# First MLP's weight words: a sign made on GpSimd, third k/v buffer pair, and q loads placed later in the plan

## The chip, the cores and the metric

One core of a Trainium2 chip runs the whole kernel. The metric is the device time of one execution in microseconds (us); three executions of the kernel before are shown and their median is used. Engines in the rows: PE is TensorE (PEld its weight loads), DVE is VectorE, ACT is ScalarE, POOL is GpSimd, SP is the engine whose queue issues nearly all DMAs.

## The reference, cut to what matters

```python
q_s = softmax(q, axis=-1)            # per row, over 64 features
k_s = softmax(k, axis=2)             # per feature, over 576 positions
kv = einsum('bhsd,bhse->bhde', k_s, v)
x = einsum('bhsd,bhde->bhse', q_s, kv)   # -> (4608, 512)
h = x @ w_in;  x = relu(h) ** 2 @ w_out          # first MLP, 512 -> 2048 -> 512
g = x @ w_gate; y = (g * sigmoid(g) * (x @ w_val)) @ w_out2   # second MLP, 512 -> 1536 -> 512
```

Batch 8, heads 8, sequence 576, head size 64. The three attention inputs are float32; the weights of both MLPs are float64 and reach the kernel as 64-bit words.

## The kernel before, in words

**Stages.** The 4608 rows are nine blocks of 512 (NB = 9). In the first half of the kernel the attention and the first MLP run block by block; the second half is the second MLP, whose products are written as seven instead of eight (the tiles `ps`, `wu`, `xo`, `uo`). Every matrix product of the MLPs is three float32r matmuls (`mm3`, L107): each operand is split into a rounded high part and the rest (`split`, L103), and high x high, high x low, low x high are added up.

**First MLP.** For block i and slice f of the 2048 hidden features (NF = 16 slices of 128) `h_mm` (L439) makes h in the PSUM tile `ph` with 12 matmuls, `g_of` (L446) makes relu squared and splits it (ScalarE: `r`, `r`, `g`; VectorE: the low half of `g`), and one slice later `acc_mm` (L454) adds the slice to the four accumulators `acc`, 12 matmuls again. So a slice is 24 matmuls.

**Weight words.** In block 0 the 32 weight slices of the first MLP (16 of `w_in`, 16 of `w_out`, 128 x 512 values of 64 bits each) are loaded, converted and split while the block is computed; later blocks find them ready. `Weights.step` (L193) is called after the prologue twice per slice f. One step does three things: `split` of the slice converted in the step before (ScalarE copy L189, GpSimd subtract L191), `bits` of the next one, and `load` (L162) of one more on SP's queue, about three steps ahead of its use. `bits_of` (L125) turns 64-bit words into float32 bit patterns: ScalarE scales the high word, read as a float32, by 2**-112 into a PSUM tile `pa` (L138); VectorE shifts it left by 3 and masks the sign bit (L140), ors in the three top bits of the low word (L144) and ors in the sign of the high word (L148, result `wbits` in SBUF). With `psum=False` the same function serves the second MLP's weights, which are converted later in blocks 1 to 7; there the intermediate tile is in SBUF. The raw words of the 32 slices are loaded into slots that the split weights take later (pools `wpa`, `wpb`); the pool `raws` (two tiles `wraw` of 4 KB a partition) is used by the second MLP's weights alone, which start in block 1.

**Attention, planned by ticks.** Work of the next block's attention is laid between the slices: the main loop calls `tick(2f)` and `tick(2f + 1)` for each f, and `attention_plan(i)` (L422) says at which tick a piece starts; a piece is a generator that advances one step per tick. For pair hp of heads (four pairs), `load_kv` (L295) loads k into the tile `kt` (one buffer) and v into `vt` (one tile), two ticks before `kv_unit` (L318), which starts at tick 2, 9, 16 or 26. `kv_unit` ends its reads of `kt` and `vt` with the 24 small matmuls of L345. `load_q` (L307) loads q into `qs` (two buffers) four ticks before `q_unit` (L359), which starts at tick 11, 12, 17 and 20, so q is loaded at ticks 7, 8, 13 and 16. The transposes `q_transpose` (L376, matmuls of L380) of pairs 0 and 1, which free the two `qs` buffers, are at ticks 14 and 16. Batch 0 and block 0 are handled by a prologue of their own (L693 to L726), with borrowed buffers.

**Order of the work.** SP's queue is issued in the order of the program (L688); an issue that must wait for a buffer holds everything behind it. The instructions of the other engines are put into an order at build time by the framework's scheduler, which looks at readiness and at the order of the program; at run time each engine works in its order and a waiting instruction holds those behind it.

Of the kernel before, what the change touches and what calls it, by code (L numbers as in the profile page):

```python
# [8 lines left out]
F32 = mybir.dt.float32  # L9
# [3 lines left out]
ALU = mybir.AluOpType  # L13
# [4 lines left out]
P = 128  # L18
# [4 lines left out]
def tile_linear_attention_two_mlps(  # L23
# [29 lines left out]
    nc = tc.nc  # L53
    B, H, S, D = q.shape
# [3 lines left out]
    T = 512  # L58
# [6 lines left out]
    CK = 96  # L65
    NC = S // CK
    LAG = 1

    def f32(ap):
        return ap.bitcast(F32)  # L70
# [15 lines left out]
    raws = ph0.enter_context(tc.tile_pool(name="raws", bufs=2, side="right"))  # L86
# [38 lines left out]
    def bits_of(raws_, psum=False):  # L125

        todo = []  # L130
        for raw in raws_:
            low, high = (
                raw.bitcast(I32).rearrange("p (n t) -> p n t", t=2)[:, :, t] for t in (0, 1)
            )
            w = cv.tile([P, T], I32, name="wbits", tag="wbits")
            todo.append((low, high, w, ps_a.tile([P, T], I32, name="pa", tag="pa") if psum else w))
        for low, high, w, t in todo:
            nc.scalar.activation(f32(t), f32(high), AF.Copy, scale=2.0**-112)  # L138
        for low, high, w, t in todo:
            nc.vector.tensor_scalar(  # L140
                t, t, 3, 0x7FFFFFFF, op0=ALU.logical_shift_left, op1=ALU.bitwise_and
            )
        for low, high, w, t in todo:
            nc.vector.scalar_tensor_tensor(  # L144
                t, low, 29, t, op0=ALU.logical_shift_right, op1=ALU.bitwise_or
            )
        for low, high, w, t in todo:
            nc.vector.scalar_tensor_tensor(  # L148
                w, high, -2**31, t, op0=ALU.bitwise_and, op1=ALU.bitwise_or
            )  # L150
        return [f32(w) for low, high, w, t in todo]

    class Weights:
# [22 lines left out]
        def bits(self, n):  # L176
            keys = self.order[self.n_bits:min(self.n_bits + n, self.n_load)]
            for key, w in zip(keys, bits_of([self.raw.pop(key) for key in keys], True)):
                self.mid[key] = w
            self.n_bits += len(keys)  # L180
# [33 lines left out]
    def operands(kind, f):  # L214
# [3 lines left out]
        for s in (f, NG + f):  # L218
            t = raws.tile([P, T], w.dtype, name="wraw", tag="wraw")
            raw_load(w, by_rows, s, t)  # L220
            raw.append(t)
        yield
        first, = bits_of(raw[:1])
        yield
        second, = bits_of(raw[1:])
        yield
        a, b = first[:, 0:U], first[:, U:2 * U]
# [50 lines left out]
    kts, qs, qT, xT = {}, {}, {}, {}  # L278

    def load_k(b, hp, t=None):  # L280
        if t is None:
            t = kp.tile([CK, 2, NC, D], F32, name="kt", tag="kt")
        nc.sync.dma_start(t, k[b, 2 * hp:2 * hp + 2].rearrange("h (p c) d -> p h c d", c=NC))
        return t

    def load_v(b, hp, t=None):
        if t is None:
            t = vt1
        for h in range(2):
            nc.sync.dma_start(  # L290
                t[:, h, :, 0:D], v[b, 2 * hp + h].rearrange("(p c) d -> p c d", c=NC)
            )
        return t

    def load_kv(b, hp):  # L295
        kts[b, hp] = load_k(b, hp), load_v(b, hp)

    def runs(i):

        done = 0  # L300
        while done < T:
            b, s = divmod(i * T + done, S)
            n = min(T - done, S - s)
            yield done // TJ, n // TJ, b, s
            done += n

    def load_q(i, hp, t=None):  # L307
        if t is None:
            t = qp.tile([P, TJ, 2, D], F32, name="qs", tag="qs")
        for p0, n, b, s in runs(i):  # L310
            for h in range(2):
                nc.sync.dma_start(
                    t[p0:p0 + n, :, h, :],
                    q[b, 2 * hp + h, s:s + n * TJ, :].rearrange("(p j) d -> p j d", j=TJ),
                )
        qs[i, hp] = t
# [42 lines left out]
    def q_unit(i, hp):  # L359

        t = qs.pop((i, hp))
        m = sp.tile([P, TJ, 2], F32, name="qm", tag="qm")
        nc.vector.tensor_reduce(m, t, axis=AX.X, op=ALU.max, negate=True)  # L363
        yield
        for j in range(TJ):
            for h in range(2):
                nc.scalar.activation(t[:, j, h], t[:, j, h], AF.Exp, bias=m[:, j, h:h + 1])  # L367
        yield
        r = sp.tile([P, TJ, 2], F32, name="qr", tag="qr")
        nc.vector.tensor_reduce(r, t, axis=AX.X, op=ALU.add)  # L370
        nc.vector.tensor_scalar(r, r, EPS, None, op0=ALU.add)
        nc.vector.reciprocal(r, r)  # L372
        nc.gpsimd.tensor_tensor(t, t, r.unsqueeze(3).to_broadcast([P, TJ, 2, D]), op=ALU.mult)  # L373
        qs[i, hp] = t

    def q_transpose(i, hp, t=None):  # L376
        pt = ps_a.tile([P, T], F32, name="pa", tag="pa")
        src = qs.pop((i, hp)).rearrange("p j h d -> p j (h d)")
        for j in range(TJ):
            nc.tensor.transpose(pt[:, j * P:(j + 1) * P], src[:, j], ident)  # L380
        if t is None:
            t = qtp.tile([P, 2, T], F32R, name="qT", tag="qT")
        split(t[:, 0], t[:, 1], pt)
        qT[i, hp] = t
# [16 lines left out]
    def run_at(plan):  # L401

        table = {}

        def add(n, fn):
            table.setdefault(n, []).append(fn)

        for n, make in plan:
            add(n, make)
        live = []  # L410

        def tick(n):
            nonlocal live
            live = [g for g in live if next(g, 0) is None]
            for make in table.get(n, ()):
                g = make()
                if g is not None and next(g, 0) is None:
                    live.append(g)

        return tick  # L420

    def attention_plan(i):  # L422

        plan = []
        if i < B:
            for hp, n in enumerate((2, 9, 16, 26)):
                plan.append((max(n - 2, 0), lambda hp=hp: load_kv(i, hp)))
                plan.append((n, lambda hp=hp: kv_unit(i, hp)))
        if i < NB:
            for hp, n in enumerate((11, 12, 17, 20)):  # L430
                plan.append((n - 4, lambda hp=hp: load_q(i, hp)))
                plan.append((n, lambda hp=hp: q_unit(i, hp)))
            plan.append((14, lambda: q_transpose(i, 0)))
            plan.append((16, lambda: q_transpose(i, 1)))
        return run_at(plan)
# [252 lines left out]
    with tc.manual_schedule(engines={mybir.EngineType.SP}):  # L688
# [4 lines left out]
        def borrowed():  # L693
            return f32(w_slot(wpb)).rearrange("p t n -> p (t n)")

        for hp in range(NP):
            kt = borrowed()[:CK, 0:2 * NC * D].rearrange("p (h c d) -> p h c d", h=2, c=NC)
            vt = borrowed()[:CK, 0:2 * NC * (D + 1)].rearrange("p (h c d) -> p h c d", h=2, c=NC)
# [3 lines left out]
        for what in "k0 k1 q0 v0 k2 q1 k3 v1 w v2 w q2 q3 w v3".split():  # L702
# [3 lines left out]
            hp = int(what[1])  # L706
# [7 lines left out]
        plan = []  # L714
# [15 lines left out]
        for n in range(NB * NF + LAG):  # L730
            i, f = divmod(n, NF)
            a = divmod(n - LAG, NF) if n >= LAG else None
            if i < NB:
                if f == 0:
                    for hp in range(NP if i else 0):
                        x_pair(i, hp)
                        if hp + 2 < NP:
                            q_transpose(i, hp + 2)
                        acc_mm(*a, hp)
                    tick = attention_plan(i + 1)  # L740
                    if i == NB - 1:
                        for _ in work:
                            pass
                        ph0.close()
                        for name, bufs in (("x1", 14), ("wr", EARLY), ("xs", 5)):
                            pools[name] = ctx.enter_context(
                                tc.tile_pool(name=name, bufs=bufs, side="right", reuse_waits="tile")
                            )
                        prime()
                        xo = XOperands(0)  # L750
                        xo.load(0)
                        for _ in range(EARLY):
                            stream.fetch()
                ph = h_mm(i, f)
                tick(2 * f)
                g_of(i, f, ph)
                if i == 0:
                    w1.step(1)
                elif i < NB - 1 and n >= NF + 2:
                    next(work, None)  # L760
# [68 lines left out]
```

## Time and profile before

| | |
|---|---|
| executions shown | 1717.01, 1717.17, 1723.07 us; median 1717.17 us |
| the profiled execution | 1724.42 us; its span 1721.9 us |
| busy in the span | PE 1687.8, DVE 919.6, ACT 861.8, POOL 253.9 us |
| first MLP's block 0, from its first steady matmuls to the end | 39 to 145 us of the span |

The rows of a trace are read as follows. A group of instructions is named by its source line, engine, operation and tiles (out<-in). A timeline row gives start, duration, count, and in brackets how long the engine was idle before and which instruction ended the wait. A row of windows gives for a stretch the busy time of each engine, the granted clock of TensorE as a share of full speed, the DMA engines' load and rate.

### The profile page before, as it was taken

How to read it: one execution, taken by the hardware profiler on the slowest of the kernel's cores; microseconds unless marked ns; L12 is line 12 of the kernel's file. 1: busy time of each engine (PE TensorE's matmuls, PEld its weight loads, DVE VectorE, ACT ScalarE, POOL GpSimd, SP SyncE). 2: the span in 40 equal slices, each digit the busy share in tenths (PEclk: the TensorE clock that was granted, in tenths of full speed). 3: DMA queues.
4: the chain of work that ended last, by engine and by line, in shares of the span. 5: the costliest groups of instructions: out<-in, count | busy, mean ns of one | idle time of the engine just before them, and what ended most of it. 6: DMA issues, size and time to landing. Idle time of an engine off the chain costs nothing.

```text
span 1721.9 us, 25446 instructions
## 1 busy us (share of the span) xinstructions
PE 1687.8 (98%) x9414; PEld 1435.6 (83%) x9414; DVE 919.6 (53%) x1626; ACT 861.8 (50%) x1719; POOL 253.9 (15%) x242
## 2 busy tenths in 40 slices
PE   5989999999999999999999999999999999999999
PEld 3668888888888888888787889988998899889999
DVE  6886555455555555544242457444755474446555
ACT  6775655555565555554343345433543354335434
POOL 2342111111110111111000210022001200121020
PEclk9999999999999999999999999999999999999999
DMA  9462443434434353333222666766776668666897
GB/s 228 136 175 78 117 132 113 144 122 125 126 109 132 113 163 104 128 105 98 80 98 93 192 216 211 237 195 213 204 247 192 208 206 250 194 201 194 254 372 281
DMA packets 192971, 292.13 MB, mean 170 GB/s; under 512 B 87248, under 2 KB 124112, under 8 KB 192848
## 3 DMA queue, kind: packets, MB, share of 16 engines
q1 hardware_dynamic: 192272, 289.46, 54.2%
q8 instruction: 75, 1.23, 0.3%
q10 hardware_dynamic: 576, 1.05, 0.2%
q14 instruction: 48, 0.39, 0.1%
HBM read 238.55 MB, written 51.90 MB: 169 GB/s over the span
## 4 chain that ended last, share of the span: by engine, by line
PE 92%; DVE 2%; issue 2%; DMA 2%; ACT 1%; POOL 1%; SPq 0%; ACTq 0%; POOLq 0%; DVEq 0%
PE ps L110 46%; PE ph L110 22%; PE acc L110 21%; PE pa L345 1%; PE pa L380 1%; POOL w L191 1%; DMA x2d<-r 1%; DMA kt<-in_k_dram 0%; DVE wbits L148 0%; DMA x<-x2d 0%; ACT r L448 0%; DVE g L105 0%; ACT r L449 0%; DVE pa L144 0%; DMA w<-in_k_dram 0%
## 5 line engine op out<-in xcount | busy, mean ns | idle before, releaser
L110 PE MATMUL ps<-xo,wu 128*128 128x512 f32 (+1 forms) x2520 | 518.6, 368 | 1.1 <-ACT ps L591 1.1
L110 PEld LDWEIGHTS ps<-xo,wu 128*128 128x128 f32 x2520 | 438.9, 189 | 79.7 <-ACT ps L591 1.5
L110 PE MATMUL acc<-g,w 128*128 128x512 f32 x1728 | 437.0, 399 | 8.6 <-ACT w L189 4.6
L110 PE MATMUL ph<-xT,w 128*128 128x512 f32 x1728 | 427.0, 395 | 4.6 <-POOL w L191 2.0
L110 PEld LDWEIGHTS ph<-xT,w 128*128 128x128 f32 x1728 | 323.4, 190 | 78.4 <-POOL w L191 4.3
L110 PEld LDWEIGHTS acc<-g,w 128*128 128x128 f32 x1728 | 318.7, 189 | 82.0 <-ACT w L189 5.9
L110 PEld LDWEIGHTS ps<-wu,uo 128*128 128x128 f32 x2268 | 272.8, 192 | 0.3
L110 PE MATMUL ps<-wu,uo 128*128 128x256 f32 x2268 | 272.9, 283 | 0.0
L105 DVE TENSOR_TENSOR g<-r,g 128x512 fp32r<-128x512 f32 x144 | 107.3, 745 | 196.2 <-ACT g L104 195.7
L448 ACT ACTIVATE r<-ph 128x512 f32<-128x512 f32 x144 | 85.9, 597 | 237.9 <-PE ph L110 234.9
L104 ACT CAST uo<-u 128x512 fp32r<-128x512 f32 (+1 forms) x210 | 120.1, 578 | 131.6 <-PE ps L110 90.6
L105 DVE TENSOR_TENSOR uo<-u,uo 128x512 fp32r<-128x512 f32 (+1 forms) x210 | 135.8, 656 | 66.1 <-ACT uo L104 65.5
L636 DVE TENSOR_TENSOR u<-u,ps 128x512 f32<-128x512 f32 (+1 forms) x60 | 38.0, 633 | 247.9 <-ACT u L635 247.9
L641 POOL TENSOR_TENSOR u<-u 128x512 f32<-128x512 f32 (+1 forms) x30 | 35.4, 1178 | 779.3 <-DVE u L637 779.3
L591 ACT COPY ps<-ps 128x512 f32<-128x512 f32 x126 | 71.8, 571 | 103.2 <-PE ps L110 100.3
L449 ACT ACTIVATE r<-r 128x512 f32<-128x512 f32 x144 | 91.0, 632 | 3.2
L104 ACT CAST g<-r 128x512 fp32r<-128x512 f32 x144 | 89.0, 618 | 3.0
L373 POOL TENSOR_TENSOR qs<-qs,qr 128x512 f32<-128x512 f32 x32 | 35.1, 1096 | 316.7 <-DVE qr L372 225.0
L367 ACT ACTIVATE qs<-qs,qm 128x64 f32<-128x64 f32 x256 | 69.3, 337 | 14.3 <-DVE qm L363 12.9
L235 POOL TENSOR_TENSOR wsum<-wbits 128x256 f32<-128x256 f32 x36 | 35.2, 990 | 244.9 <-DVE wbits L148 237.2
L635 ACT ACTIVATE u<-ps 128x512 f32<-128x512 f32 (+1 forms) x60 | 33.3, 555 | 53.0 <-PE ps L110 52.8
L600 ACT COPY p<-ps 128x512 f32<-128x512 f32 x63 | 37.0, 587 | 42.6 <-PE ps L110 41.7
(100 smaller groups left out, 1347.6 us busy)
## 6 DMA issues: line engine op xcount, KB each, us to landing
wu<-gvd SPq DMA_DIRECT2D x210, 512.0 KB, 4.3
wu<-od SPq DMA_DIRECT2D x105, 512.0 KB, 4.5
gvd<-wst SPq DMA_DIRECT2D x84, 256.0 KB, 2.3
od<-wst SPq DMA_DIRECT2D x42, 256.0 KB, 2.3
w<-in_moe_w_in_dram SPq DMA_DIRECT2D x16, 512.0 KB, 6.4
w<-in_moe_w_out_dram SPq DMA_DIRECT2D x16, 512.0 KB, 5.9
x<-x2d SPq DMA_DIRECT2D x32, 256.0 KB, 5.4
kt<-in_k_dram SPq DMA_DIRECT2D x28, 288.0 KB, 3.4
```

Of the source, the lines that this page charges most:

```text
L104: nc.scalar.copy(hi, src)
L105: (eng or nc.vector).tensor_tensor(lo, src, f32(hi), op=ALU.subtract)
L110: nc.tensor.matmul(ps, lhsT=w[s], rhs=x[t], start=start and n == 0, stop=stop and n == 2, skip_group_check=more,)
L235: nc.gpsimd.tensor_tensor(to, x, y, op=op)
L367: nc.scalar.activation(t[:, j, h], t[:, j, h], AF.Exp, bias=m[:, j, h:h + 1])
L373: nc.gpsimd.tensor_tensor(t, t, r.unsqueeze(3).to_broadcast([P, TJ, 2, D]), op=ALU.mult)
L448: nc.scalar.activation(r, ph, AF.Relu)
L449: nc.scalar.activation(r, r, AF.Square)
L591: nc.scalar.copy(x, y)
L600: nc.scalar.copy(x, y)
L636: nc.vector.tensor_tensor(u, u, gate, op=ALU.mult)
L641: nc.gpsimd.tensor_tensor(s1, a21, a22, op=ALU.add)
```

## The change

`bits_of` with `psum=True` (the first MLP alone) gets a path of its own: GpSimd multiplies the high word, read as float32, by 0.0 in place, which leaves its sign alone in the word; VectorE then does two passes, shift left and or with that sign, and or with the low word's three bits. The mask pass is gone and the separate sign pass is merged. For batch 1 (the second) and pairs 1 and 3, `load_kv` takes two tiles of the pool `raws` for k and v instead of `kt` and `vt`, and GpSimd writes the column of ones into the v tile (96 x 12 values). In the plan of every block, q of pair 2 is loaded at tick 15 instead of 13 and its unit starts at 18 instead of 17; q of pair 3 is loaded at tick 17 instead of 16, unit at 20 as before.

```diff
         for low, high, w, t in todo:
             nc.scalar.activation(f32(t), f32(high), AF.Copy, scale=2.0**-112)
+        if psum:
+
+            for low, high, w, t in todo:
+                nc.gpsimd.tensor_scalar(f32(high), f32(high), 0.0, None, op0=ALU.mult)
+            for low, high, w, t in todo:
+                nc.vector.scalar_tensor_tensor(
+                    t, t, 3, high, op0=ALU.logical_shift_left, op1=ALU.bitwise_or
+                )
+            for low, high, w, t in todo:
+                nc.vector.scalar_tensor_tensor(
+                    w, low, 29, t, op0=ALU.logical_shift_right, op1=ALU.bitwise_or
+                )
+            return [f32(w) for low, high, w, t in todo]
...
     def load_kv(b, hp):
-        kts[b, hp] = load_k(b, hp), load_v(b, hp)
+        kt = vt = None
+        if b == 1 and hp % 2:
+
+            kt, vt = (
+                raws.tile([P, T], w_in.dtype, name="wraw", tag="wraw").bitcast(F32) for _ in range(2)
+            )
+            kt = kt[:CK, 0:2 * NC * D].rearrange("p (h c d) -> p h c d", h=2, c=NC)
+            vt = vt[:CK, 0:2 * NC * (D + 1)].rearrange("p (h c d) -> p h c d", h=2, c=NC)
+            nc.gpsimd.memset(vt[:, :, :, D:D + 1], 1.0)
+        kts[b, hp] = load_k(b, hp, kt), load_v(b, hp, vt)
...
-            for hp, n in enumerate((11, 12, 17, 20)):
-                plan.append((n - 4, lambda hp=hp: load_q(i, hp)))
+            for hp, (l, n) in enumerate(((7, 11), (8, 12), (15, 18), (17, 20))):
+                plan.append((l, lambda hp=hp: load_q(i, hp)))
                 plan.append((n, lambda hp=hp: q_unit(i, hp)))
```

## Rows read from the trace of the kernel before

**Rows 1.** The page: busy time of PE, share of the span, instructions.
```profile
PE 1687.8 (98%) x9414; PEld 1435.6 (83%) x9414; DVE 919.6 (53%) x1626; ACT 861.8 (50%) x1719; POOL 253.9 (15%) x242
```

**Rows 2.** Windows: the stage before 39 us, block 0, its worst part, block 1.
```profile
0.00:39.00 39.00, 22.44 (x144) 14.63 (x144) 25.97 (x64) 22.81 (x62) 6.86 (x17) 1.00 0.98 238
...
100.00:115.00 15.00, 12.21 (x38) 8.26 (x39) 11.63 (x21) 10.42 (x23) 5.30 (x4) 0.77 0.98 286
...
39.00:145.00 106.00, 96.80 (x472) 72.71 (x473) 86.69 (x154) 76.02 (x158) 46.54 (x35) 0.95 0.49 140
...
150.00:175.00 25.00, 25.00 (x133) 20.32 (x133) 12.50 (x24) 12.48 (x22) 3.25 (x4) 1.00 0.36 101
```

**Rows 3.** Timeline of PE from 78 to 122 us: start, duration, instruction, idle before.
```profile
78.09 0.96 PE L110 MATMUL acc<-g,w 128*128 128x512 f32 x3 [1.56 <-ACT w L189]
...
85.75 0.92 PE L345 MATMUL pa<-vt,kt 96*64 96x65 f32 x24
...
101.86 2.83 PE L110 MATMUL acc<-g,w 128*128 128x512 f32 x5 [2.85 <-ACT w L189]
...
105.10 3.28 PE L110 MATMUL acc<-g,w 128*128 128x512 f32 x7
108.22 0.27 PE L333 MATMUL pa<-ident,mx 128*96 128x128 f32 x1
...
111.46 0.96 PE L110 MATMUL acc<-g,w 128*128 128x512 f32 x3 [0.22 <-ACT w L189]
112.83 2.34 PE L110 MATMUL acc<-g,w 128*128 128x512 f32 x9 [0.41 <-POOL w L191]
...
118.80 2.88 PE L110 MATMUL acc<-g,w 128*128 128x512 f32 x12
121.52 2.88 PE L110 MATMUL ph<-xT,w 128*128 128x512 f32 x12
```

**Rows 4.** Waits of SP's queue up to 170 us: total, times, longest.
```profile
SPq L283 <- PE pa L345: 30.8, 3, 14.9
...
SPq L312 <- PE pa L380: 17.5, 1, 17.5
```

**Rows 5.** Timeline of SP's queue from 72 to 94 us: start, time to issue, DMA.
```profile
72.46 0.65 SPq L120 DMA_DIRECT2D w<-in_moe_w_in_dram  x1
90.62 2.52 SPq L312 DMA_DIRECT2D qs<-in_q_dram  x4
93.18 0.61 SPq L118 DMA_DIRECT2D w<-in_moe_w_out_dram  x1
93.85 0.42 SPq L283 DMA_DIRECT2D kt<-in_k_dram  x1
```

**Rows 6.** Timeline of DVE: a wait, two passes in a row, a stretched instruction.
```profile
101.72 0.55 DVE L323 TENSOR_TENSOR m<-kt 96x384 f32<-96x384 f32 x1 [3.35 <-DMA kt<-in_k_dram]
...
125.37 0.69 DVE L140 TENSOR_SCALAR pa<-pa 128x512 int32<-128x512 int32 x1
125.97 0.68 DVE L148 SCALAR_TENSOR_TENSOR wbits<-w,pa 128x512 int32<-128x512 int32 x1
...
139.56 1.61 DVE L105 TENSOR_TENSOR g<-r,g 128x512 fp32r<-128x512 f32 x1
```

**Rows 7.** Groups by shape, first 150 us: busy us, mean ns, idle before.
```profile
L191 POOL TENSOR_TENSOR w<-wbits,w 128x512 fp32r<-128x512 f32 x32 | 43.1, 1351 | 64.9 <-ACT w L189 64.9
...
L140 DVE TENSOR_SCALAR pa<-pa 128x512 int32<-128x512 int32 x32 | 22.0, 690 | 2.7 <-ACT pa L138 2.5
...
L189 ACT CAST w<-wbits 128x512 fp32r<-128x512 f32 x32 | 19.4, 613 | 6.9 <-DVE wbits L148 6.9
...
masks.py:199 POOL TENSOR_SCALAR_AFFINE_SELECT ident<-ident 128x128 f32<-128x128 f32 x1 | 0.3, 296 | 0.0
...
masks.py:197 POOL MEMSET ident<- 128x128 f32 x1 | 0.2, 204 | 0.3 <-POOLq L811 0.3
```

**Rows 8.** Timeline of POOL: the subtract beside the stretched instruction of rows 6.
```profile
138.81 1.82 POOL L191 TENSOR_TENSOR w<-wbits,w 128x512 fp32r<-128x512 f32 x1 [2.77 <-ACT w L189]
```

## Prediction

> **What bounds the kernel now.** I read the busy times first: PE is busy for 1687.8 of 1721.9 us [rows 1], so the whole kernel can lose at most 34 us to waiting, and the question is where those lie. The windows answer it. From 150 us on a window of 25 us holds 25.00 us of PE [rows 2]; up to 39 us PE has 22.44 of 39, while the prologue waits for its first inputs. Between them lies block 0 of the first MLP, in which the weight words are converted: 96.80 us of PE in 106, at a granted clock of 0.95. That is 9.2 us idle, and a mean of 0.95 between the two levels 2.4 and 1.2 GHz means that a tenth of the stretch ran at 1.2, which costs 106 x 0.05 = 5.3 us more. So **14.5 us** are lost in the one stretch that the change touches. What is gained there arrives at the end in full, because PE behind it is never short of work.
>
> The timeline of PE shows the largest piece [rows 3]. At 101.86 PE has been idle for 2.85 us, and the next twelve matmuls last until 108.22, that is 6.36 us. Twelve undisturbed ones take 2.72 us (118.80 to 121.52). Two smaller waits follow at 111.46 and 112.83 (0.22 and 0.41), in the wake of the first. Together 2.85 + 3.64 + 0.63 = 7.1 us; of it I take off 0.2 for a small transpose that falls into it, which leaves 6.9. In this part the granted clock is 0.77 [rows 2]: PE had gone idle, and its clock fell to 1.2 GHz after that.
>
> PE waits there for a weight's copy on ScalarE, but the cause sits on SP's queue [rows 4, 5]. After the weight load of 72.46 nothing is issued until 90.62: the q load of pair 2 waits 17.5 us for the transposes of pair 0 to free its buffer, with two weight loads and the k load of pair 2 behind it. Then 2.52 us of q, a weight load and, at 93.85, k are issued almost at once. VectorE comes to k's first maximum, has to wait 3.35 us for it until 101.72 [rows 6], and the passes over weight words stand behind that instruction. So a late k, not a slow engine, opens the hole.
>
> **The change, part by part.**
>
> *q loads later.* Pair 2's four q DMAs move from tick 13 to 15, behind two weight loads and the k and v loads of pair 2; pair 3's move from 16 to 17, behind one weight load. The q load still waits for the transposes until about 90, but what is now ahead of it no longer does. Behind it stand the weight loads of ticks 15 and 16, which are needed some three steps later; they go out as the queue comes free, two or three us of issue behind q's 2.52. Pair 2's unit starts a tick later too, so its q has as many ticks as pair 3's, three, to land. In blocks 1 to 7 the same moves change SP's order, but PE has no holes there [rows 2]; I cost them at nothing. That cover would be gone only if q came after the next block's first use, which is over ten ticks away.
>
> *Two more buffers.* Alone, the move would let k of pair 2 run into the next wait: the single k tile is read until the matmuls of pair 1 end at 85.75 + 0.92 = 86.7 [rows 3], and SP's queue would stand there instead. With pairs 1 and 3 in buffers of their own, pair 2 finds its tile free since pair 0's unit. So k can be issued at about 74 instead of 93.85, and 3.35 us of VectorE's waiting go with it. The 30.8 us that k loads wait in three places [rows 4] are for the most part later and hidden. The added fills of ones on GpSimd are two tiny ones (fills of 128 x 128 take 204 ns, rows 7, and these are a tenth of that); nothing. The two tiles are needed by the second MLP's weights only in block 1. These two parts together are worth the hole: **-6.9 us**, between 0 (if the burst of loads is late in another place) and -7.1.
>
> *Two passes instead of three.* Every word slice loses one VectorE pass of 690 ns [rows 7], which in a row costs 0.60 (125.37 to 125.97, rows 6). About 29 of the 32 fall into block 0's stretch: 29 x 0.60 = 17.4 us off the 86.69 that VectorE is busy in 106 [rows 2], from 82% to 65%. GpSimd takes 29 sign passes over 128 x 512 values, every second word, in place. No row shows that instruction. From below, a fill of 128 x 128 takes 204 ns and four times that is 0.82; from above, the two-input subtract of the same size takes 1.35; the one-input select of 128 x 128, 296 ns, times four would be 1.18, with its fixed part counted four times. I take 0.85, as one input is nearest to the fill and the select without that fixed part, and keep 0.30 (as if the length cost nothing) to 1.35 as ends. GpSimd goes from 46.54 to 46.54 + 29 x 0.85 = 71.2 us, below ScalarE's 76.02 [rows 2], so it does not become the bound by its sum.
>
> The Trainium skill has a price for one input (GPSIMD Engine Reference, section 3.1): 769 ns for 512 elements at best; by it GpSimd's sum would be an estimated 46.54 + 22.3 = 68.8 us. No row here shows that instruction.
>
> What is the relief worth? It can only fill the rest of the hole: 14.5 - 6.9 = 7.6 us, such as the 1.56 us at 78.09, where PE waits for the same copy of a weight [rows 3]. That chain is ScalarE, VectorE, ScalarE, GpSimd, and only one of the links gets shorter, while a new GpSimd link of 0.85 takes the place of the 0.60. So latency of a single word gets 0.25 us worse and throughput gets better. Ends: +10.3 (rival B) and -7.6; I take a third, **-2.5 us**.
>
> A cost against it shows in the trace: the subtract of g at 139.56, with both inputs in SBUF, took 1.61 us while a GpSimd subtract that started at 138.81 ran for 1.82 [rows 6, 8]; more GpSimd time means more of these. About 14 such subtracts of g lie in the stretch; with sign passes running for a quarter of the time and half a pass to wait for, that is 14 x 0.25 x 0.43 = 1.5 us of VectorE, against 17.4 saved. That is why I take a third and not a half. The Trainium skill (SBUF — State Buffer, section "Who interferes with whom") states the rule: a VectorE instruction with two SBUF inputs and a GpSimd instruction that reads SBUF shut each other out for a whole instruction. The row agrees.
>
> **The sum.** -6.9 - 2.5 = -9.4 us. Against the profiled execution (span 1721.9, 1724.42 with what lies around it) that is 1715.0. That execution stands 7.25 us above the median of 1717.17, so the forecast for a median is 1717.17 - 9.4 = **1708 us** to the nearest us, with a range of its own from 1702 to 1714.
>
> **The rivals.**
>
> *A. VectorE's time is waited away again.* The two remaining passes stand behind the sign pass, and if VectorE reaches them before GpSimd is done, it waits in its order with the split of g behind it. By the lock that the rows show, 29 passes could cost VectorE up to 29 x 0.85 = 24.7 us if every one of them hit, more than the 17.4. For it: GpSimd now visits each word twice. Against it: 64.9 us of GpSimd's idle time lie just before its subtracts [rows 7], so there is room. Then only the loads' gain stays, 1717.17 - 6.9 = 1710.3, or half of it, 1713.7. I put 1712. The Trainium skill's rule (SBUF — State Buffer, section "Who interferes with whom"), if every pass hit, would make it 24.7 - 17.4 = 7.3 us worse than the loads alone, which is no change.
>
> *B. Slower: GpSimd's order makes a chain.* The step's subtract of word j stands ahead of the sign of word j + 1. If the order of the engines keeps the words strictly in turn, a word's period is copy 0.61, subtract 1.35, sign 0.85 and two passes 1.20, 4.01 us [rows 6, 7]. Block 0's 29 words now take 106 us, 3.65 each; from that period on the chain decides. It gives 29 x 4.01 = 116.3, +10.3, so 1727; with the sign at 1.35 it would be 29 x 4.51 = 130.8 and 1742. Against it: raw words are there three steps ahead and there are two PSUM tiles, so that the sign of one word can run before the subtract of the last.
>
> *C. The hole closes altogether.* All 14.5 us come back, 1702.7. For it: VectorE at 65%. Against it: ScalarE, with 76.02 us in the stretch, keeps all its work, and any idle time of PE that is left can take the clock with it, as at 101.86.
>
> *D. The loads do nothing.* k of pair 2 lands in time, but weight loads of ticks 15 and 16 behind the q load are now the late ones, and the hole moves by a few us. Then only the 2.5 remain: 1714.7.
>
> **How the numbers follow.** Forecast 0.45, of which 0.33 lies below 1708.6 (0.5% under the median; 0.5% is about what a measurement of this kernel can tell from no change) and 0.12 above; A 0.22; B 0.11; C 0.14; D 0.08. Faster: 0.33 + 0.14 = 0.47. Same: 0.12 + 0.22 + 0.08 = 0.42. Slower: 0.11. The range from 1702 to 1718 takes in the forecast, A, D and most of C, and leaves out B and the end of C, below 0.2.
>
> **What would show it.** Right: k of pair 2 issued near 74 us, no DVE wait for it, PE without the idle time near 100 and a granted clock of 1.00 there, DVE near 70 us in block 0's stretch, sign passes of 0.8 to 0.9 us. Wrong: sign passes above 1.2 us, DVE waits named after GpSimd's sign, PE waits for weights in every slice, or block 0 ending at 145 us or later. The forecast fails as a whole if the hole at 101.86 is gone and PE's idle time turns up elsewhere before 145 us.

## The result: slower by 0.8%, and the profile after

The median is **1732.48 us** (1731.64 to 1735.43, four runs) against 1718.88 for before (1717.01 to 1723.07, four runs beside them). The ratio is 1.0082, with a 95% interval from 1.0065 to 1.0098. The forecast was 1708 in a range from 1702 to 1718, so the sign was wrong and the range missed. The profiled execution took 1735.43 us, with a span of 1733.6.

The busy line of the page and the windows of the kernel after, which answer to [rows 1] and [rows 2] (the fourth window goes to the end of block 0, which is now at 158.60, and the last is from 145 to 175):

```profile
PE 1690.0 (97%) x9414; PEld 1440.0 (83%) x9414; DVE 900.7 (52%) x1594; ACT 862.0 (50%) x1719; POOL 301.5 (17%) x276
```

```profile
0.00:39.00 39.00, 21.96 (x144) 14.61 (x144) 25.35 (x62) 23.30 (x63) 11.45 (x21) 1.00 0.96 239
100.00:115.00 15.00, 10.41 (x42) 7.81 (x41) 10.55 (x18) 8.14 (x16) 10.31 (x7) 0.89 0.46 133
39.00:145.00 106.00, 87.47 (x393) 67.39 (x394) 68.50 (x114) 66.86 (x142) 84.10 (x60) 0.89 0.49 141
39.00:158.60 119.60, 101.07 (x473) 78.34 (x473) 76.93 (x128) 75.20 (x157) 91.32 (x65) 0.90 0.44 125
145.00:175.00 30.00, 30.00 (x165) 24.81 (x164) 16.12 (x28) 17.63 (x32) 7.22 (x5) 1.00 0.22 70
```

Against [rows 2], VectorE has 68.50 us in the stretch from 39 to 145 in place of 86.69, and GpSimd 84.10 in place of 46.54. Not all of VectorE's difference is relief: the stretch now holds less of block 0 (393 matmuls in place of 472). Up to the block's end VectorE has 76.93 us, and over the whole span it lost 32 instructions and 919.6 - 900.7 = 18.9 us. PE went the wrong way: from 39 us to the end of the block it idles for 119.60 - 101.07 = 18.5 us, where it was 9.2, and its granted clock is 0.90 in place of 0.95. No engine is full in the stretch from 39 to 145, GpSimd with 84.10 of 106 included. So this isn't an engine that ran out of time; the next views show work waiting for work.

The timeline of PE after (start, duration, instruction, idle before and releaser), beside [rows 3]:

```profile
77.44 0.42 PE L350 MATMUL pa<-ident,m 96*128 96x96 f32 x1 [3.80 <-DVE wbits L148]
77.56 5.04 PE L110 MATMUL acc<-g,w 128*128 128x512 f32 x11
...
107.89 1.11 PE L402 MATMUL pa<-ident,qs 128*128 128x128 f32 x4 [4.17 <-DVE wbits L148]
...
135.45 5.06 PE L110 MATMUL acc<-g,w 128*128 128x512 f32 x11 [2.83 <-DVE g L105]
...
158.60 1.11 PE L110 MATMUL ph<-qT,kv 128*128 128x64 f32 x6
```

The hole at 101.86 is gone, and other holes have come all along the block: 3.80 us, 4.17, 2.83. Behind each the matmuls are stretched (eleven in 5.04 us, where twelve undisturbed ones took 2.72). Behind the first the granted clock is 0.50, that is the lower level, 1.2 GHz (window after):

```profile
77.56:82.40 4.84, 4.84 (x12) 3.65 (x13) 1.80 (x4) 3.60 (x11) 1.94 (x2) 0.50 1.06 351
```

Block 0 ends where the first matmuls of block 1's x start, at 158.60; in the timeline of PE before, the same instruction stood at 145.13:

```profile
145.13 1.11 PE L110 MATMUL ph<-qT,kv 128*128 128x64 f32 x6
```

The **13.5 us** between them are close to the difference of the medians, 13.6. The two profiled executions differ by only 1735.43 - 1724.42 = 11.0 us, mostly since the one of before loses more behind block 0 (see the part on the loads below). From 145 to 175 us PE is never idle (30.00 of 30).

The waits of all engines after, from 20 to 160 us (who, for whom, total, times, longest):

```profile
DVE pa L144 <- POOL w L142: 27.9, 25, 2.9
ACT w L202 <- DVE wbits L148: 23.1, 13, 3.2
POOL w L204 <- ACT w L202: 18.5, 12, 2.7
POOL w L142 <- ACT pa L138: 12.7, 5, 3.7
...
PE pa L402 <- DVE wbits L148: 4.2, 1, 4.2
...
PE pa L350 <- DVE wbits L148: 3.8, 1, 3.8
```

L142 is the new sign pass on GpSimd, L144 and L148 the two VectorE passes, L202 ScalarE's copy and L204 GpSimd's subtract. Read downwards it is a ring: VectorE waits for GpSimd's sign, ScalarE for VectorE, GpSimd for ScalarE. The sign in its turn overwrites the word that ScalarE reads first, hence the 12.7. VectorE was given 18.9 us of free time and spends 27.9 waiting for the sign. What stands behind such a wait shows at 133.65 (timeline of VectorE after):

```profile
133.65 0.70 DVE L144 SCALAR_TENSOR_TENSOR pa<-pa,w 128x512 int32<-128x512 int32 x1 [2.50 <-POOL w L142]
134.26 1.14 DVE L105 TENSOR_TENSOR g<-r,g 128x512 fp32r<-128x512 f32 x1
```

This g is the one that PE waits for until 135.45.

The chain of waits after, from 39 to 160 us, as shares of those 121 us by line:

```profile
by line: PE acc L110 17.9%; POOL w L142 17.5%; issue 17.0%; PE ph L110 10.9%; POOL w L204 8.5%; DVE pa L144 5.7%; DVE wbits L148 4.3%; DMA qs<-in_q_dram 2.9%; POOL qs L395 2.5%; PE pa L402 1.2%; DVE m L346 1.1%; DVE qr L392 1.1%; DVE g L105
```

The sign pass alone makes up 17.5% of it, 21.2 us. One stretch of it, from the timeline of all engines after:

```profile
72.97 3.10 POOL L142 TENSOR_SCALAR w<-w 128x512 f32<-128x512 f32 x2
...
74.59 0.70 DVE L144 SCALAR_TENSOR_TENSOR pa<-pa,w 128x512 int32<-128x512 int32 x1 [0.20 <-POOL w L142]
...
76.03 1.27 POOL L204 TENSOR_TENSOR w<-wbits,w 128x512 fp32r<-128x512 f32 x1
76.10 0.70 DVE L144 SCALAR_TENSOR_TENSOR pa<-pa,w 128x512 int32<-128x512 int32 x1 [0.81 <-POOL w L142]
...
76.70 1.27 DVE L148 SCALAR_TENSOR_TENSOR wbits<-w,pa 128x512 int32<-128x512 int32 x2
77.44 0.42 PE L350 MATMUL pa<-ident,m 96*128 96x96 f32 x1 [3.80 <-DVE wbits L148]
```

Two words are converted in one go. GpSimd needs 3.10 us for their signs; VectorE takes one word up after the first, waits 0.81 for the second, and only then come the passes at L148. PE's transpose writes a PSUM tile `pa`, of the same two that hold the words between ScalarE's first instruction and L148. So PE, with its 3.80 us, waits for a tile that a word keeps while its sign is made. How much of the loss goes by way of these tiles, no run separates.

The groups by shape after, first 160 us (count, busy us, mean ns, idle before), which answer to [rows 7]:

```profile
L142 POOL TENSOR_SCALAR w<-w 128x512 f32<-128x512 f32 x32 | 50.9, 1597 | 12.8 <-ACT pa L138 12.7
L204 POOL TENSOR_TENSOR w<-wbits,w 128x512 fp32r<-128x512 f32 x32 | 43.4, 1362 | 20.4 <-ACT w L202 18.5 <-DMA w<-in_moe_w_in_dram 1.9
```

The sign pass takes **1.60 us**, more than the two-input subtract of the same size and above the upper end of 1.35. The queue of SP after, beside [rows 5]:

```profile
74.65 0.37 SPq L296 DMA_DIRECT2D kt<-in_k_dram  x1
...
96.71 3.72 SPq L334 DMA_DIRECT2D qs<-in_q_dram  x4
100.48 0.60 SPq L118 DMA_DIRECT2D w<-in_moe_w_out_dram  x1
```

k of pair 2 goes out at 74.65 (93.85 before), and none of VectorE's waits is for k. That half did what was forecast. The q load of pair 2, forecast for about 90, goes out at 96.71, behind transposes that are themselves late (PE has them at 95.99).

### The profile page after: what moved, and what is told of

Its sections match the earlier page's. It is cut to its first block, busy times and chain, and to the rows that moved or that the text cites. A ratio compares the mean times of both kernels' runs of the same rounds, so it can differ in the third digit from the quotient of the medians.

```text
span 1733.6 us, 25425 instructions
## 1 busy us (share of the span) xinstructions
PE 1690.0 (97%) x9414; PEld 1440.0 (83%) x9414; DVE 900.7 (52%) x1594; ACT 862.0 (50%) x1719; POOL 301.5 (17%) x276
## 4 chain that ended last, share of the span: by engine, by line
PE 90%; DVE 3%; POOL 2%; issue 2%; DMA 1%; ACT 1%; SPq 0%; ACTq 0%; POOLq 0%; DVEq 0%
PE ps L110 45%; PE acc L110 21%; PE ph L110 21%; POOL w L142 1%; PE pa L367 1%; PE pa L402 1%; POOL w L204 1%; DMA x2d<-r 1%; DVE pa L144 0%; DMA x<-x2d 0%; DVE wbits L148 0%; DVE g L105 0%; PE pa L350 0%; DMA w<-in_k_dram 0%; DVE qr L392 0%
```

## The experiments

The theory: the loads gain what they should, and GpSimd's sign pass costs more than everything else brings, since VectorE waits for it in its order. The rivals: the loads brought nothing; GpSimd is simply too busy, whoever waits for it; or the price of the one instruction is the whole of it. All medians stand against those of before measured beside them, from 1718.28 to 1718.89.

### The two halves apart

The change without its loads (`load_kv` and `attention_plan` of before), and the change without its two-pass block (no `if psum:` block).

> Only the new passes over the weight words, with the k, v and q loads of before. Theory 1 (a sign pass of 1.54 us fills GpSimd's queue, 2.9 us a word with the subtract, and VectorE, ScalarE and TensorE wait behind it): slower than before by 12 to 22 us, 1731 to 1741, no better than the whole change, VectorE waiting for the sign pass some 25 us in block 0. Theory 2 (the loads placed later cost the time, the passes are harmless): within 4 us of before, 1715 to 1723.

> Only the loads: two more buffers for k and v, q of pairs 2 and 3 later; the three passes of before. Theory 1: faster than before by about the 6.9 us that the prediction gave these parts, 1709 to 1714, TensorE without the 2.85 us wait near 100 us. Theory 2: slower by 8 to 14 us, 1727 to 1733, as the whole change.

The sign pass alone: 1740.07, ratio 1.0126 (1.0111 to 1.0141). The loads alone: 1714.39, ratio 0.9977 (0.9967 to 0.9986), just above the range of its first theory. So the halves have opposite signs, and the harm is in the sign half. The waits of VectorE in the kernel with the sign pass alone, from 20 to 160 us:

```profile
DVE pa L144 <- POOL w L142: 31.8, 26, 2.9
```

The window of block 0 and the queue of SP in the kernel with the loads alone:

```profile
39.00:145.00 106.00, 99.28 (x513) 76.08 (x512) 90.43 (x163) 78.69 (x163) 46.45 (x36) 1.00 0.49 143
```

```profile
70.71 0.38 SPq L283 DMA_DIRECT2D kt<-in_k_dram  x1
...
88.50 3.02 SPq L321 DMA_DIRECT2D qs<-in_q_dram  x4
```

The loads fill the hole: a clock of 1.00, and block 0 ends at 138.39, 6.7 us sooner than in the profile of before.

### Which of the two load edits it is

```diff
-            for hp, n in enumerate((11, 12, 17, 20)):
-                plan.append((n - 4, lambda hp=hp: load_q(i, hp)))
+            for hp, (l, n) in enumerate(((7, 11), (8, 12), (15, 18), (17, 20))):
+                plan.append((l, lambda hp=hp: load_q(i, hp)))
```

These lines alone on before, and on the other hand the two k and v buffers alone (`load_kv` of the change).

> Only the q loads of pairs 2 and 3 later; one k and one v buffer, three passes. By the prediction, k of pair 2 then waits for the single k tile until pair 1's matmuls end at 86.7 instead of 90.6 for q, so little is gained: 1715 to 1720. If the q order is the whole of the loads' gain: 1713 to 1715, as both together.

> Only the two more buffers; q loads and passes as before. By the prediction k of pair 2 still stands behind q on SP's queue until 93.9, so nothing is gained: 1716 to 1720. If the buffers are the gain: 1713 to 1715.

The q move alone: 1714.86, ratio 0.9976 (0.9967 to 0.9986). The buffers alone: 1719.18, 0.9999 (0.9990 to 1.0008). The q move is the whole gain, and the buffers add nothing to it (1714.39 with both): what held k back was q at the head of SP's queue. The second wait that I expected behind it, for pair 1's k tile, does come in the kernel with the q move alone (queue of SP):

```profile
85.32 0.33 SPq L283 DMA_DIRECT2D kt<-in_k_dram  x1
```

It costs nothing by itself: at 85.32 k is still in time, and VectorE takes it up at 90.97 without a wait.

### The price of the instruction

In the kernel with the loads alone, a row of seven forms was run twice on an unused tile, ahead of its first use:

```python
nc.gpsimd.tensor_scalar(odd, odd, 0.0, None, op0=ALU.mult)      # L710, every second word, in place
nc.gpsimd.tensor_scalar(left, left, 0.0, None, op0=ALU.mult)    # L711, contiguous, in place
nc.gpsimd.tensor_scalar(right, left, 0.0, None, op0=ALU.mult)   # L712, contiguous, to another place
# L713 and L714: L710 and L711 over 256 columns
nc.gpsimd.tensor_copy(right, left)                              # L715
nc.gpsimd.tensor_tensor(right, left, left, op=ALU.subtract)     # L716
```

> The loads alone, with GpSimd passes of several forms before its first use, each twice, to measure them by themselves: 128 x 512 with every second word in place, contiguous in place, contiguous to another half, 128 x 256 of both, a copy and a two-input subtract. If the word step makes the price: 1.5 us with the step, 0.7 to 0.9 without, and 0.8 for half the length with the step. If any one-input scalar pass has that price: 1.5 us in all three of full length, above the two-input subtract's 1.28.

Groups by shape of GpSimd, first 20 us (one run, 1722.13 us in all with the probes):

```profile
L710 POOL TENSOR_SCALAR wraw<-wraw 128x512 f32<-128x512 f32 x2 | 3.3, 1634 | 0.1
L712 POOL TENSOR_SCALAR wraw<-wraw 128x512 f32<-128x512 f32 x2 | 3.0, 1490 | 0.2
L711 POOL TENSOR_SCALAR wraw<-wraw 128x512 f32<-128x512 f32 x2 | 3.0, 1490 | 0.2
L716 POOL TENSOR_TENSOR wraw<-wraw 128x512 f32<-128x512 f32 x2 | 2.1, 1039 | 0.2
L713 POOL TENSOR_SCALAR wraw<-wraw 128x256 f32<-128x256 f32 x2 | 1.8, 890 | 0.2
L714 POOL TENSOR_SCALAR wraw<-wraw 128x256 f32<-128x256 f32 x2 | 1.7, 849 | 0.2
L715 POOL COPY wraw<-wraw 128x512 f32<-128x512 f32 x2 | 1.2, 611 | 0.1
```

The multiply by a constant is the slow form: 1.49 us, where a copy takes 0.61 and a two-input subtract 1.04 (of a tile from itself; the kernel's own subtract, of two tiles, takes 1.36). In place or not makes no difference, and the step over every second word little (the two of L710 took 1.53 and 1.74).

### No sign pass at all

The whole change with the sign taken by the second VectorE pass and nothing on GpSimd, which leaves out the three low bits; and the same on before's loads:

```diff
-            for low, high, w, t in todo:
-                nc.gpsimd.tensor_scalar(f32(high), f32(high), 0.0, None, op0=ALU.mult)
             for low, high, w, t in todo:
-                nc.vector.scalar_tensor_tensor(t, t, 3, high, ...)
+                nc.vector.tensor_scalar(t, t, 3, 0x7FFFFFFF, ...)
             for low, high, w, t in todo:
-                nc.vector.scalar_tensor_tensor(w, low, 29, t, ...)
+                nc.vector.scalar_tensor_tensor(w, high, -2**31, t, op0=ALU.bitwise_and, op1=ALU.bitwise_or)
```

> The loads of the change and two VectorE passes without any sign pass: the shift, and the sign taken from the high word. The three low bits of each weight are left out of the computation. It measures what one VectorE pass less is worth when no other engine pays for it. By the prediction's step: 2.5 us under the loads alone, 1710 to 1713. If VectorE was no limit once the loads are in time: 1713.5 to 1716. If most of the rest of the hole was VectorE's: below 1709.

> The two passes without a sign pass and without the three low bits, with the loads of before: the control for the next run. The relief measured with the new loads was 5.2 us; if it adds up with the loads: 1711 to 1716. If the late k of before hides it: 1716 to 1720.

With the loads: 1709.22, ratio 0.9942 (0.9929 to 0.9955). On before's loads: 1712.45, 0.9955 (0.9940 to 0.9970). The window of block 0 in the first:

```profile
39.00:145.00 106.00, 100.74 (x532) 80.22 (x531) 78.95 (x134) 78.50 (x164) 43.04 (x35) 1.00 0.53 151
```

Both kernels have as many VectorE passes per word as the change. So the sign pass on GpSimd, and it alone, costs 1732.48 - 1709.22 = **23.3 us** with the loads, and 1740.07 - 1712.45 = 27.6 without. The relief of VectorE is worth 1714.39 - 1709.22 = 5.2 us with the loads and 6.3 without.

### The dose, and the sign on other terms

The two-pass block for every second word (`if psum and self_n():`, which is true every second time); the sign made by ScalarE, by an activation with scale 0.0 in place of the GpSimd line; and the sign made on GpSimd with a second input, a column of zeros, in place of the constant:

```diff
-                nc.gpsimd.tensor_scalar(f32(high), f32(high), 0.0, None, op0=ALU.mult)
+                nc.gpsimd.tensor_tensor(f32(high), f32(high), zeros.to_broadcast([P, T]), op=ALU.mult)
```

The column was put among the constants first, then, in a kernel of its own, behind all the other tiles, so that those ahead of it stay where they were.

> The whole change, but only every second weight slice takes the new passes; the others keep the three of before. GpSimd would have 46 + 15 x 1.54 = 69 us of 106. If the harm starts only where GpSimd is full: 1708 to 1717. If each sign pass costs its share: half way between 1714.4 and 1732.5, 1721 to 1726.

> The whole change, but ScalarE makes the sign, in place, with a scale of 0.0 (0.63 us). GpSimd is as loaded as before. If GpSimd's time is the cause: most of the 14 us come back, but ScalarE goes from 79 to about 95 us of the 106, so 1712 to 1722. If the two-pass form itself is the cause: 1727 to 1735.

> The whole change, but the sign is a two-input multiply with a column of zeros, which took 1.04 us alone where the scalar form took 1.53. If GpSimd's time per word decides: 1.04 + 1.3 = 2.35 us a word is well below the 3.65 us that a word has, so the time falls to 1706 to 1716, at or below the loads alone (1714.4). If any sign pass between ScalarE and VectorE does the harm, whatever its length: 1723 to 1732.

> The whole change with the two-input sign of 1.05 us again, its column of zeros now at the end of another pool, so that no other tile lies at another place. In the first version block 0 ended 10 us earlier than with the scalar form but the second MLP's matmuls of 512 columns took 229 ns each instead of 223. If the place of the tiles did that: 223 again and 1723 to 1728 in all, about half of the harm. If the sign's form does not matter: 1731 to 1736.

Half of the words: 1719.56, ratio 0.9998 (0.9989 to 1.0008). That falls between the two expectations. It is 5.2 us above the loads alone, where all the words are 18.1 above. Twice the dose cost three and a half times as much; the waits grow 2.6 times, from 10.9 to 27.9 (waits of VectorE with half the words, 20 to 150 us):

```profile
DVE pa L150 <- POOL w L148: 10.9, 12, 1.4
```

The sign on ScalarE: 1714.79, ratio 0.9973 (0.9962 to 0.9984), the same as the loads alone. This kernel does not compute the reference's function, so it stands here for its time only. The relief of VectorE (77.65 us) is there, and is taken back: VectorE waits 12.2 us for ScalarE's sign, and ScalarE is now busy for 93.02 of 106 us:

```profile
39.00:145.00 106.00, 100.27 (x504) 78.68 (x505) 77.65 (x134) 93.02 (x192) 45.02 (x36) 0.95 0.50 144
```

The two-input sign with the column behind the other tiles: 1724.01, ratio 1.0032 (1.0019 to 1.0044). Group and wait of that kernel:

```profile
L144 POOL TENSOR_TENSOR w<-w,zeros 128x512 f32<-128x512 f32 x32 | 35.8, 1128 | 13.4 <-ACT pa L140 13.3
```

```profile
DVE pa L146 <- POOL w L144: 17.3, 20, 2.4
```

With 1.13 us in place of 1.60, 8.5 of the 23.3 us are gone. So the price matters, and the rival that it is the whole of the harm falls: at 1.13 us, inside my bounds, the change is still slower than before. The kernel with the column among the constants took 1734.3, ratio 1.0081 (1.0066 to 1.0096), above both of its expectations, though its block 0 ended at 148.68, as early as the other's 148.33; its 10 us more come later and are told in the last section.

### Busy or waited for

If GpSimd is just too busy, a pass that nobody reads must cost the same. Three kernels add such a pass, and a fourth keeps the sign pass but needs it later.

The first adds to before an unread multiply over every second word of a tile of its own; the second adds to before an unread multiply over the finished word; the third adds the same to the two-pass kernel on before's loads:

```diff
+            for low, high, w, t in todo:
+                nc.gpsimd.tensor_scalar(idle, f32(w), 0.0, None, op0=ALU.mult)
```

The fourth has before's three VectorE passes, with the sign pass ahead of them; its result is read by the third.

> The kernel before, plus one GpSimd pass of the same form for each weight slice over a tile of its own that nobody reads: GpSimd is as loaded as in the changed kernel, VectorE keeps its three passes and waits for no sign. Theory 1a (GpSimd's load alone does it, by late subtracts): slower by 8 to 20 us, 1727 to 1739. Theory 1b (it needs VectorE's wait in its order behind the sign pass): within 5 us of before, 1716 to 1724.

> The kernel before, plus one GpSimd scalar pass for each weight slice over its finished bits into a tile that nobody reads; it stands in GpSimd's order between the bits and the subtract. VectorE keeps three passes and waits for no GpSimd result of a word. If GpSimd's fullness with late subtracts is enough: slower by 8 to 20 us, 1726 to 1738. If VectorE's wait in its order is needed: 1715 to 1723.

> The control plus one GpSimd scalar pass a word over the finished bits, into a tile nobody reads: GpSimd as full as in the run with the sign alone (1740), its subtracts late by a pass, but VectorE waits for no result of GpSimd. If GpSimd's fullness and the late subtracts are all of it: 1733 to 1741. If VectorE's wait in its order is the larger part: 1717 to 1724, some 6 us over the control, as the idle pass cost over the kernel before.

> The kernel before with the sign pass on GpSimd added, but VectorE keeps three passes and needs the sign for the third alone, some 1.2 us later in its order than in the change. If VectorE's wait is the larger part: its wait for the sign falls well under 31.8 us and the time is under 1736 although VectorE does a pass more. If GpSimd's fullness decides: 1740 to 1750.

The first can't be used: 1754.1, ratio 1.0213 (1.0197 to 1.0228), but its passes depend on nothing, so the order that was built puts them first of all. Its window up to 39 us has GpSimd busy for 36.70 and PE for 5.80, and PE waits for the normalising of q behind them (waits of PE, 20 to 160 us):

```profile
0.00:39.00 39.00, 5.80 (x55) 3.90 (x55) 13.20 (x33) 9.45 (x26) 36.70 (x36) 1.00 0.96 237
```

```profile
PE pa L384 <- POOL w L377: 36.9, 3, 22.1
```

The other three answer the question. Group and window of the two-pass kernel with the unread pass:

```profile
L151 POOL TENSOR_SCALAR wraw<-wbits 128x512 f32<-128x512 f32 x32 | 49.5, 1548 | 23.5 <-DVE wbits L147 21.8 <-DVE rd L365 1.2
```

```profile
39.00:145.00 106.00, 95.36 (x491) 73.01 (x492) 75.77 (x128) 75.26 (x158) 90.47 (x65) 1.00 0.46 138
```

Waits of VectorE in the kernel whose third pass reads the sign, 20 to 160 us:

```profile
DVE wbits L151 <- POOL w L141: 5.6, 9, 0.9
```

| on before's loads | VectorE passes | GpSimd's added pass | us | ratio to before (95%) |
|---|---|---|---|---|
| two passes alone | 2 | none | 1712.45 | 0.9955 (0.9940 to 0.9970) |
| unread pass | 2 | 1.55 us, nobody waits | 1718.04 | 0.9993 (0.9984 to 1.0003) |
| sign pass alone | 2 | 1.58 us, first pass waits | 1740.07 | 1.0126 (1.0111 to 1.0141) |
| before | 3 | none | 1718.7 | 1 |
| unread pass | 3 | 1.56 us, nobody waits | 1725.21 | 1.0033 (1.0021 to 1.0044) |
| sign read last | 3 | 1.66 us, third pass waits | 1730.05 | 1.0057 (1.0036 to 1.0079) |

The unread pass makes GpSimd busier than the whole change does (90.47 of 106 against 84.10) and costs 5.6 us, or 6.3 beside three passes (1725.21 against 1718.89). The same pass costs 27.6 where VectorE's first pass needs it. Needed two passes later it costs 11.3, and VectorE's waits for it shrink from 31.8 to 5.6, though VectorE works a pass more per word. So a fuller GpSimd, with its subtracts late, is about a fifth of the harm. The unread pass comes behind the word, though, not ahead of it. The kernel that reads the sign last has the pass ahead, as the change has, and costs 11.3; so at most 11.3 of the 27.6 us go with GpSimd's load and the pass's place in its queue, and some 16 with its being read first. What this leaves open: that kernel has three VectorE passes and not two, so the split is not an exact one.

The fastest kernel here, 1709.22, leaves out bits. The fastest that computes all of it is the q move, alone (1714.86) or with the buffers (1714.39), which beats both kernels.

## Why the prediction was wrong

**The step that failed** is the sign pass, in two terms: its price, and the latency that it adds to a word, which I put at 0.25 us and let the relief outweigh. For the price I took 0.85 us from the fill and the select, between ends of 0.30 and 1.35; it took 1.60 in the kernel and 1.53 and 1.74 by itself. The upper end was the two-input subtract, on the belief that one input can't cost more than two. The probe shows the opposite for this form: 1.49 with one input and a constant, 1.04 with two, 0.61 for a plain copy. The copy came out below my figure, the multiply far above it.

The price is not the whole of it. The sign pass cost 23.3 us at 1.60 us a word and 1724.01 - 1709.22 = 14.8 at 1.13. A straight line through the two, which is an estimate and a rough one, gives 9.7 us at the 0.85 that I took: even at that price the change would have come out near 1719, with no gain.

The Trainium skill's 769 ns for 512 elements at best (GPSIMD Engine Reference, section 3.1) led the same way; the probe's 1490 for the multiply differs and decides, and its 611 for the copy lies below it.

**"It does not become the bound by its sum"** was true and beside the point. GpSimd has 84.10 of 106 us and idles before its own instructions. An engine in the middle of a word's way need not be full to set its pace. I weighed this as rival B, with the right mechanism: GpSimd's subtract and sign in turn, and a word's period above 3.65 us. I gave it 0.11 for the reason that raw words are there three steps ahead and that there are two PSUM tiles. The trace shows why that was weak: in the stretch from 72.97 the signs of a pair of words and VectorE's passes over them come back to back, so being ahead buys nothing inside the pair, and attention's transposes want the two tiles too (the 3.80 and 4.17 us of PE). The period became (158.60 - 39)/29 = 4.12 us. B's formula with the measured parts, 0.61 + 1.36 + 1.60 + 1.20 = 4.77, is the strict chain; the block moved 42% of the way to it from 3.65. B's 1727 was the nearest of all my cases to 1732.48. Rival A, at 0.22, had the other half of the mechanism: VectorE waits in its order for the sign, with the split of g behind it. It let that wait eat no more than the loads had left, 1712, because GpSimd's 64.9 us of idle time before its subtracts looked like room; the wait came to 27.9 us. The lock that A also priced is not what did it: the two passes took 0.70 and 0.68 us each, about as long as a pass before (0.69).

**What is late next** was missing in the sum. I costed the latency of a word at 0.25 us and then let 17.4 us of VectorE's freed time weigh more. In its order the first VectorE pass now stands behind GpSimd, and what stands behind it waits too: 2.83 us of PE at 135.45 are for such a split of g.

**Loads, -6.9:** right in mechanism, too large in size: -3.9 (1714.39 against 1718.28). In the profiles block 0 ends 6.7 us earlier, as forecast, but the profiled execution of before took 1724.42, which is 5.5 above the median of 1718.88, and I had the term from it. Part of that excess lies elsewhere: from the end of block 0 to the end of the span it takes 1721.9 - 145.13 = 1576.8 us, the kernel with the loads alone 1712.4 - 138.39 = 1574.0, at granted clocks of 0.98 and 1.00 from 800 to 1000 us. That the hole itself was larger than usual in that execution is argued, not shown. The q move carries all of it and the buffers none: the wait for pair 1's k tile, named as the reason for them, cost nothing when q was moved alone. Rival D falls.

**Relief of VectorE, -2.5:** too small; it measured -5.2. By accident the two errors cancel: without the sign pass the change takes 1709.22, 9.5 us less than its before, where the sum was -9.4. The whole miss is the sign pass, +23.3.

**The stretching of VectorE's two-input subtracts**, put at 1.5 us: the g subtracts went from a mean of 820 ns to 880, but the two-pass kernel without any sign pass shows 887, so it can't be put down to the sign pass. Nothing of the result needs it.

**Of the signs named ahead:** k near 74 us (74.65), no wait for k, and VectorE near 70 (68.50) came as written, the last in part because less of the block lies in the stretch. A granted clock of 1.00 from 100 us on did not come (0.89). Sign passes above 1.2 us, VectorE's waits named after the sign, and block 0 ending at 145 or later came from the list of what would make it wrong, and so did the sign of a failure as a whole: the hole at 101.86 is gone, and PE's idle time turned up elsewhere before 145 us.

## What to carry to other kernels

Work that is moved to an idle engine in the middle of a dependent chain is priced by its latency and by what stands behind the instruction that waits for it, not by the sum of the engine's busy time: here the same pass cost 5.6 us unread, 11.3 read late and 27.6 read first. If it has to be moved, let the last consumer need it, and check which shared buffers are held meanwhile. An upper bound from "the same engine with more inputs" is no bound when the form of the instruction is another; where no row has the form, widen the end that decides the sign.

## What the hardware showed that was not expected

GpSimd's multiply by a constant over 128 x 512 takes 1.49 us, more than twice a copy (0.61) and half as much again as a two-input subtract of a tile from itself (1.04); over 256 columns it takes 0.85, so a fixed part of some 0.2 us and 2.5 ns per column (worked out from the two).

Adding one column of four bytes per partition to the constants, ahead of the other tiles in SBUF, made matmuls of the second MLP slower. Groups by shape of PE from 900 us to the end, first with the column among the constants, then with it behind the other tiles:

```profile
L113 PE MATMUL ps<-xo,wu 128*128 128x512 f32 x2016 | 469.3, 395 | 0.5 <-ACT ps L616 0.5
```

```profile
L112 PE MATMUL ps<-xo,wu 128*128 128x512 f32 x2016 | 458.0, 389 | 0.7 <-ACT ps L615 0.7
```

That is 11.3 us over 2016 matmuls, at a granted clock of 1.00 in both (the window from 1000 to 1025 us holds 109 matmuls with the column ahead and 112 with it behind). That the place of the tiles is the cause is argued from the sources, which differ only in where the column is made, and why it should act was not tried; the kernel after, which adds no tile of its own, has the same 458.0 as before.
